# Order of the up and down products, preparation distance and number of tile places in a Fourier and mixture-of-experts kernel

## The chip, the core and the metric

The kernel runs on one core of one Trainium2 chip. The metric is the device time of one execution in microseconds. The core has five engines with a queue each: PE (matrix products; PEld are its weight loads), ACT and DVE (elementwise work and the emptying of the product banks), POOL (elementwise work, and the issue of the indirect gathers and scatters) and SP (which here only issues DMAs). Each engine takes its own instructions strictly in the order in which the program lists them, and engines wait for each other through semaphores.

## What is computed

```python
X = np.fft.rfft(x, axis=1)                      # x: 8 x 2496 x 256
Yr = Xr @ w_r - Xi @ w_i + b_r
Yi = Xr @ w_i + Xi @ w_r + b_i
Yr, Yi = soft_threshold(Yr, 0.01), soft_threshold(Yi, 0.01)
y = np.fft.irfft(Yr + 1j * Yi, n=2496, axis=1)  # 19968 tokens of 256
e_idx = np.argmax(y @ w_gate, axis=1)           # 8 experts
for e in range(8):
    mask = e_idx == e
    h = np.maximum(y[mask] @ w1[e], 0.0)        # 256 -> 1024
    out[mask] = gate_w[mask, None] * eom[mask, e, None] * (h @ w2[e])
```

## The kernel before

The Fourier part works through the eight sequences one after another: two stages of the forward transform, the mixing with the weights, two stages of the inverse, whose rows go to a DRAM buffer `yd`. Its last product stages are line 761 (first inverse stage, reads `zhl`) and line 827 (last inverse stage, reads `bdt`, the transposed `bt`; its results pass through `yt` and are stored by line 847).

The expert part works on tiles of 128 tokens that share an expert. There are 163: tiles 0 to 63 come from the first four sequences and are paired, 32 blocks of two tiles of one expert; tiles 64 to 162 are blocks of one tile. A tile goes through these steps, each with its line:

- `gathers`, line 1327: POOL issues an indirect gather of the tile's rows into a place `yg`.
- `tokens`, lines 1343 to 1353: DVE and ACT scale the rows and split them into two 16-bit parts in a place `yhl`.
- `tokens`, line 1366: SP issues a DMA transpose of `yhl` into a place `eT`. This ends what is called preparing a tile.
- `up`, line 1458: PE multiplies with the expert's first matrix, in pieces; ACT (1468) and DVE (1469) empty each piece into `hh`.
- `down`, line 1424: PE multiplies with the second matrix; ACT (1440) empties the product into `o`, and POOL scatters it (1443).

Expert weights lie in three buffers `wbuf`, which the blocks use in turn (the first four blocks use two). `fetch`, line 1313, has SP issue two DMAs of 1 MB for every block: the first part (for `up`) once the up product of the block three before is done, the second (for `down`) once the down product of that block is done. Both are conditional: a register that SP reads first (line 1310) says whether the buffer already holds this expert, and then the DMA moves nothing. So most tiles load nothing, and at a change of expert three blocks in a row load both parts.

The order on every engine is written by a planner (`Issue`): coroutines ask for an engine with a priority, which is the second item of what they yield, and of those that are ready in the plan the lowest goes first. `Slots` and `Places` are counted resources: a coroutine waits in the plan until one is free, and the real waits (semaphores) follow from the memory that the instructions touch. `AHEAD` holds a tile's preparation back in the plan until the up product of the tile so many before is planned. `down` for a single tile asks for PE with priority 4 after its tile's `up`, where the next tile's `up` stands at 5.6.

Of the kernel before, what the change touches and what calls it, by code (L numbers as in the profile page):

```python
# [13 lines left out]
F16 = mybir.dt.float16  # L14
F32 = mybir.dt.float32
# [9 lines left out]
B, S, D, E, DF = 8, 2496, 256, 8, 1024  # L25
N = B * S
N1, N2, K1 = 39, 64, 20
NQ = 22
P3 = 3 * N1
NCOL = B * NQ  # L30
ROW = 260
LAM = 0.01
XR = 6
# [3 lines left out]
T_A = -((-(NA * S - E * 255)) // 256) * 2  # L37
# [107 lines left out]
TAIL = 1.7  # L145
# [3 lines left out]
PLACES = dict(yg=6, yhl=5, eT=3, hh=2, o=5)  # L149
UP, DN = 2.8, 1.4  # L150
AHEAD = 6
KW = 4
YR, ZR, AN, WR, SR = 2, 3, 6, 3, 6
S1 = 6
# [15 lines left out]
OL = 2, 3  # L170
# [115 lines left out]
def tile_fft_moe(ctx, tc, x, w_r, w_i, b_r, b_i, w_gate, w_og, w1, w2, f1, f4, cmat, gmat, m16, out, dbg=None):  # L286
    nc = tc.nc
# [146 lines left out]

    bt = pf.tile([128, 4 * NQ, 128], F16, name="bt")
    G.memset(bt[:, :, 120:], 0.0)

    ste = pf.tile([128, 2, 2, 120], F32, name="ste")
    G.memset(ste, 0.0)
    bdt = py.tile([128, 4 * NQ, 128], F16, name="bdt")  # L440
    at = pm.tile([128, K1, 2, 2, 128], F16, name="at")
# [9 lines left out]
    io = Issue(list(range(8)))  # L451
    slots = {k: Slots(n) for k, n in dict(x=XR - 6, s1=S1, A=AN, xt=3, z=2, zhl=ZR, bt=1, bd=1, yt=YR, ol0=OL[0], wr=WR - 1, wsp=SR, ol1=OL[1], fac=12, dg=1, gL=1).items()}
    slots.update({k: Places(range(EARLY[k])) for k in EARLY})
# [3 lines left out]
    def move(r, nbytes, issue, fn):  # L457

        yield "S", r, max(issue, nbytes / RATE), fn
# [817 lines left out]
    def open_h():  # L1277
# [6 lines left out]
        for k, n in PLACES.items():  # L1284
            for i in range(EARLY[k], n):
                io.put(slots[k], i)

    def place(k, i, shape, dt):
        return pools["w" if i < EARLY[k] else "h"].tile(shape, dt, tag=f"{k}{i}", name=f"{k}{i}")

# [7 lines left out]
    def fetch(r):  # L1298

        yield "w open"  # L1300
        for k, (t, n) in enumerate(BLOCKS):
            yield "plan", 0 if t < T_A else 1
            if k == KW:
                yield "opened"
            for m in range(2):
                if before(k) is not None:
# [22 lines left out]

    facs = psm.tile([128, 18], F32, name="facs")  # L1330
    yms = psm.tile([128, 8], F32, name="yms")

    def tokens(t, iy, yg, r):

        il = yield slots["yhl"]
        yield slots["fac"]
        if t >= AHEAD:
            p = t - AHEAD
            yield "up", p - p % 2 if p < T_A else p
        m = yms[:, t % 8:t % 8 + 1]  # L1340
        fac = facs[:, t % 18:t % 18 + 1]
        yhl = place("yhl", il, [128, 2, 256], F16)
# [10 lines left out]
        yield "D", r - 10, 0.48, lambda: V.scalar_tensor_tensor(yhl[:, 1], yg[:, :256], s, yhl[:, 0], ALU.mult, ALU.subtract)  # L1353
        io.put(slots["yg"], iy)
        if t >= T_A:
# [9 lines left out]
        eT = st["eT", t][1][:, t % 2 if t < T_A else 0]  # L1365
        yield from move(r - 10, 1.4e5, 1.2, lambda: nc.sync.dma_start(eT.rearrange("p v c n -> p (v c) n"), yhl.rearrange("p v d -> p (v d)"), transpose=True))
        st["fac", t] = fac
        yield TAIL
        io.put(slots["yhl"], il)
        io.set("eT", t)  # L1370
# [9 lines left out]
    def back(k, t, i):  # L1380

        if t >= T_A:
            io.put(slots[k + "1"], i)
            return
        st["n" + k] = st.get("n" + k, 0) + 1
        if st["n" + k] <= T_A // 2 - PLACES[k]:
            io.put(slots[k], i)
        else:
            for h in range(2):
                io.put(slots[k + "1"], (i, h))  # L1390

    def block(k, r):
# [18 lines left out]
        for i in range(m):  # L1411
            io.go(down(t + i, m, i, w, hh, ih, r + (11.2 + 2 * UP * i + DN if m > 1 else 4)))

    def down(t, m, n, w, hh, ih, r):
# [28 lines left out]
        yield "G", r - DN, 1.0, lambda: G.indirect_dma_start(out=outs[t % 8], out_offset=bass.IndirectOffsetOnAxis(ap=sidx[:, t:t + 1], axis=0), in_=o, in_offset=None, bounds_check=N - 1, oob_is_err=False)  # L1443
        yield 3.6
        io.put(slots["o"], io_)
# [48 lines left out]
    io.go(open_w())  # L1494
    io.go(open_h())
    io.go(fetch(P * B + RT + WF))
    io.go(gathers(P * B + RT))
# [28 lines left out]
```

## Time and profile before

| | us |
|---|---|
| median of three timed runs | 1444.25 |
| the three runs | 1444.25, 1450.45, 1444.25 |
| profiled execution, own time | 1450.28 |
| span of the profiled execution | 1448.5 |
| PE busy in it | 1402.4 |
| DVE, ACT, POOL busy in it | 978.5, 737.0, 636.1 |
| first up product starts at | 552.01 |
| up products of single tiles from about | 907 |

The span is from the first to the last instruction of that execution; its own time is 1.78 us longer. Engine rows of a timeline give the start, the duration, the line, the operation, the tiles and a count; in square brackets the idle time ahead of the row and what ended it. A PE row's duration runs some 0.16 us into the row behind it, since products overlap; the time that a row occupies is the distance to the next row's start.

### The profile page before, as it was taken

To read this page: it belongs to the slowest core of one execution; us is meant where nothing else is said; L and a number is where in the kernel's file an instruction comes from. 1 tells how busy PE (TensorE), PEld (TensorE's weight loads), DVE (VectorE), ACT (ScalarE), POOL (GpSimd) and SP (SyncE) were. 2 spreads that over 40 slices of the span, in tenths; PEclk is the share of its full clock that TensorE was granted. 3 is DMA by queue.
4 is the path that set the end of the run, shared out by engine and by line. 5 is a ranking of instruction groups with operands and counts; after the bars stand their busy time and mean duration, and the time that the engine had idled before them with its cause. 6 is when DMAs were issued, how large, how long until landed. Compare 5 with 4: busy or idle time off the path is not lost.

```text
span 1448.5 us, 42626 instructions
## 1 busy us (share of the span) xinstructions
PE 1402.4 (97%) x16436; PEld 1273.4 (88%) x16436; DVE 978.5 (68%) x2796; ACT 737.0 (51%) x1413; POOL 636.1 (44%) x729
## 2 busy tenths in 40 slices
PE   4999999999999999999999999999999999999998
PEld 4998887888888888888888888999999999989998
DVE  4888767788998896788888855545545455445452
ACT  4777675778687764433333333333333333333342
POOL 2274565355577563345554333333343333333321
PEclk8999999999999999999999999999999999999999
DMA  7779899998988789977795789674838568386520
GB/s 197 174 174 217 205 224 211 220 223 216 218 211 202 177 238 197 285 193 199 232 231 145 215 207 264 168 218 111 245 94 227 160 167 242 81 244 194 126 58 24
DMA packets 294005, 276.47 MB, mean 191 GB/s; under 512 B 241847, under 2 KB 250169, under 8 KB 282026
## 3 DMA queue, kind: packets, MB, share of 16 engines
q1 hardware_dynamic: 277239, 229.68, 62.5%
q0 software_dynamic: 15872, 42.83, 12.3%
q8 instruction: 129, 2.11, 0.6%
q10 hardware_dynamic: 690, 1.24, 0.3%
q14 instruction: 75, 0.61, 0.1%
HBM read 337.44 MB, written 58.91 MB: 274 GB/s over the span
## 4 chain that ended last, share of the span: by engine, by line
PE 45%; issue 29%; POOL 14%; DVE 6%; DMA 2%; ACT 2%; SPq 1%; POOLq 0%; ACTq 0%; DVEq 0%
PE ps L731 11%; PE ps L1458 9%; PE ps L1424 8%; POOL out L1443 7%; POOL yg L1327 7%; PE ps L623 5%; PE ps L761 3%; PE ps L827 3%; PE ps L701 3%; DMA x<-in_x 1%; PE ps L872 1%; PE ps L666 1%; PE ps L725 1%; PE ps L1253 1%; DVE z L747 1%
## 5 line engine op out<-in xcount | busy, mean ns | idle before, releaser
L1458 PE MATMUL ps<-eT,wbuf 128*128 128x128 f16 (+1 forms) x6288 | 460.9, 233 | 8.4 <-DMA wbuf<-wd 5.6
L1424 PE MATMUL ps<-wbuf,hh 128*128 128x256 f16 x3912 | 453.8, 273 | 0.6 <-DMA wbuf<-wd 0.6
L1458 PEld LDWEIGHTS <-wbuf 128*128 128x128 f16 x6288 | 419.2, 98 | 30.0 <-DMA wbuf<-wd 7.2
L1424 PEld LDWEIGHTS <-hh 128*128 128x128 f16 x3912 | 378.9, 98 | 45.7 <-issue 1.3
L1469 DVE SCALAR_TENSOR_TENSOR hh<-ps,hh 128x512 f16<-128x512 f32 x326 | 224.9, 690 | 275.8 <-ACT hh L1468 275.6
L1468 ACT ACTIVATE hh<-ps 128x512 f16<-128x512 f32 x326 | 194.6, 597 | 294.3 <-PE ps L1458 287.9
L1443 POOL DMA_INDIRECT out<-o,sidx x163 | 163.4, 1003 | 283.4 <-ACT o L1440 259.7
L1327 POOL DMA_INDIRECT yg<-yd,gidx x163 | 161.5, 991 | 252.4 <-DVE yhl L1353 218.2
L731 PE MATMUL ps<-whl,xt 128*128 128x256 f16 x1920 | 223.1, 273 | 0.7 <-ACT xt L716 0.7
L731 PEld LDWEIGHTS <-xt 128*128 128x128 f16 x1920 | 187.6, 98 | 32.2 <-ACT xt L716 1.1
L1440 ACT ACTIVATE o<-ps,facs 128x256 f32<-128x256 f32 x163 | 77.2, 473 | 229.1 <-PE ps L1424 138.4
L1353 DVE SCALAR_TENSOR_TENSOR yhl<-yg,ys,yhl 128x256 f16<-128x256 f32 x163 | 81.8, 508 | 66.2 <-ACT yhl L1352 66.1
L623 PEld LDWEIGHTS ps<-f1t,x 117*128 117x128 f32 (+1 forms) x704 | 86.4, 199 | 18.2 <-issue 15.9
L623 PE MATMUL ps<-f1t,x 117*128 117x120 f32 (+1 forms) x704 | 89.9, 284 | 0.2 <-ACT ste L778 0.2
L1352 ACT ACTIVATE yhl<-yg,ys 128x256 f16<-128x256 f32 x163 | 81.7, 501 | 13.9 <-DVE ys L396 6.2
L751 POOL TENSOR_TENSOR zhl<-z,zhl 128x512 f16<-128x512 f32 x54 | 62.7, 1162 | 52.4 <-ACT zhl L749 50.0
L1028 POOL TENSOR_TENSOR wsp<-wr,wsp 128x512 f16<-128x512 f32 x62 | 74.3, 1198 | 5.2
L761 PE MATMUL ps<-gt,zhl 128*128 128x128 f16 x960 | 65.7, 220 | 7.9 <-DVE zhl L751 3.4
L761 PEld LDWEIGHTS <-zhl 128*128 128x128 f16 x960 | 58.6, 98 | 15.0 <-DVE zhl L751 4.2
L827 PE MATMUL ps<-bdt,f4t 120*117 120x512 f16 x264 | 70.6, 383 | 0.1
L632 ACT ACTIVATE at<-ps,sx 128x480 f16<-128x480 f32 (+1 forms) x88 | 55.7, 650 | 29.1 <-PE ps L623 25.9
L633 DVE SCALAR_TENSOR_TENSOR at<-ps,sx,at 128x480 f16<-128x480 f32 (+1 forms) x88 | 59.3, 696 | 12.5 <-ACT at L632 12.3
(195 smaller groups left out, 1647.8 us busy)
## 6 DMA issues: line engine op xcount, KB each, us to landing
wbuf<-wd SPq DMA_DIRECT2D x262, 1024.0 KB
yd<-yt SPq DMA_DIRECT2D x120, 158.4 KB
x<-in_x SPq DMA_DIRECT2D x114, 156.0 KB
wr<-in_moe_w SPq DMA_DIRECT2D x32, 512.0 KB
wd<-wsp SPq DMA_DIRECT2D x64, 256.0 KB
yg<-yd,gidx POOLq DMA_INDIRECT x163
eT<-yhl SPq DMA_TRANSPOSE x163
out<-o,sidx POOLq DMA_INDIRECT x163
```

The source lines that it names most:

```text
L623: T.matmul(pv[:, dh, :, m * j:m * j + m], xs[:k, j0 + j, 128 * dh:128 * dh + 128], fw, start=True, stop=True)
L731: T.matmul(yp[:, 256 * j:256 * j + 256], xt_[:, v, 2 * dh + j, 64 - 64 * u:192 - 64 * u], whl[:, dh, vw, 256 * u:256 * u + 256], start=Fal ...
L761: T.matmul(bv[:, j], zhl[:, vz, c:c + 128], gt[:, 2 * p + j, v], start=(n == 0), stop=(n == 2))
L827: T.matmul(pt[:P3], w, src[:, :, :, vb_], start=(n == 0), stop=(n == 2))
L1327: yield "G", r + 5.6 * t - 30, 1.0, lambda: G.indirect_dma_start(out=yg, out_offset=None, in_=src, in_offset=bass.IndirectOffsetOnAxis(ap= ...
L1352: yield "A", r - 10, 0.5, lambda: A.activation(yhl[:, 0], yg[:, :256], AF.Copy, scale=s)
L1353: yield "D", r - 10, 0.48, lambda: V.scalar_tensor_tensor(yhl[:, 1], yg[:, :256], s, yhl[:, 0], ALU.mult, ALU.subtract)
L1424: T.matmul(st["pt", t][1][:, :256], hh[:, v, fc, 128 * n:128 * n + 128], w[:, fc // 2, vw, fc % 2], start=(fc == k == 0), stop=(fc == 7 an ...
L1443: yield "G", r - DN, 1.0, lambda: G.indirect_dma_start(out=outs[t % 8], out_offset=bass.IndirectOffsetOnAxis(ap=sidx[:, t:t + 1], axis=0), ...
L1458: T.matmul(pt[:, 128 * m * j:128 * m * (j + 1)], w[:, dh, g // 4, vw, 128 * (g % 4):128 * (g % 4) + 128], eT[:, :m, v, dh], start=(n == 0) ...
L1468: yield "A", r, 0.6, lambda: A.activation(hv[:, 0], pt, AF.Relu)
L1469: yield "D", r, 0.69, lambda: V.scalar_tensor_tensor(hv[:, 1], pt, 0.0, hv[:, 0], ALU.max, ALU.subtract)
```

## The change

It does four things. A single tile's down product gets priority 8 in place of 4, behind the next tile's up product and ahead of that of the tile after it. The distance at which tiles are prepared, 6 before, becomes 8 for tiles 0 to 27, 14 for tiles 28 to 63 and 12 for the single tiles. The Fourier part's `bt` and `bdt` are reused, once the last inverse transform has been stored, as 13 more places for `yg`, 8 for `yhl`, 6 for `eT` and 8 for `o` (`open_late`). And a few rules of the plan change: the second block's weights are asked for only when the second tile is prepared, the transposes of the first four tiles get an early priority, and places are given back in the plan a little later.

```diff
-AHEAD = 6
+AHEAD = 8, 8, 14, 12
+LATE = dict(yg=13, yhl=8, eT=6, o=8)
+FAR = 28
...
+    def open_late():
+        yield "ys", B - 1, 5
+        yield "btr", B - 1
+        yield "lbm", B - 1
+        yield "opened"
+        room = []
+        for pool, tag in ((pf, "bt"), (py, "bdt")):
+            room.append((pool.tile([128, 4 * NQ * 128], F16, tag=tag, name="late" + tag), [0]))
+        for k, size in (("o", 512), ("yhl", 512), ("eT", 1024), ("yg", 2 * ROW)):
+            for i in range(PLACES[k], PLACES[k] + LATE[k]):
+                w, at_ = next(x for x in room if x[1][0] + size <= 4 * NQ * 128)
+                late[k, i] = w[:, at_[0]:at_[0] + size]
+                at_[0] += size
+                io.put(slots[k], i)
...
             if k == KW:
                 yield "opened"
+            if k == 1:
+                yield "eT", 1
...
-        if t >= AHEAD:
-            p = t - AHEAD
+        p = t - AHEAD[2 * (t >= FAR) + (t >= T_A)]
+        if p >= 0:
             yield "up", p - p % 2 if p < T_A else p
...
-        io.put(slots["yg"], iy)
+        io.at(io.now + (4 if t > 11 else 0), io.put, slots["yg"], iy)
...
-        yield from move(r - 10, 1.4e5, 1.2, lambda: nc.sync.dma_start(eT..., yhl..., transpose=True))
+        yield from move(r - (10 if t > 3 else 70), 1.4e5, 1.2, lambda: nc.sync.dma_start(eT..., yhl..., transpose=True))
...
-            io.go(down(t + i, m, i, w, hh, ih, r + (11.2 + 2 * UP * i + DN if m > 1 else 4)))
+            io.go(down(t + i, m, i, w, hh, ih, r + (11.2 + 2 * UP * i + DN if m > 1 else 8)))
...
-        yield 3.6
+        yield 8.0
         io.put(slots["o"], io_)
```

What this does to the order shows at three places. First ACT among the single tiles. Its rows stand for PE's products: two rows of line 1468 (1495 in the changed kernel) empty one tile's up product, one row of 1440 (1467) a down product; 1352 (1379) prepares a tile. Before:

```order
L1468 ACTIVATE hh0_9904<-ps1_16894 128x512
L1468 ACTIVATE hh0_9904<-ps4_16921 128x512
L1352 ACTIVATE yhl1_16946<-yg4_16236,ys4_16972 128x256
L1468 ACTIVATE hh0_9904<-ps6_16977 128x512
L1440 ACTIVATE o0_17073<-ps0_17006,facs_146 128x256
L1352 ACTIVATE yhl2_17031<-yg5_16349,ys5_17043 128x256
L1440 ACTIVATE o1_17128<-ps7_17048,facs_146 128x256
```

And in the changed kernel, in the same part of the program:

```order
L1495 ACTIVATE hh1_9953<-ps6_16454 128x512
L1495 ACTIVATE hh1_9953<-ps7_16486 128x512
L1379 ACTIVATE latebt_11351<-yg4_15365,ys7_16563 128x256
L1467 ACTIVATE o4_16598<-ps4_16532,facs_146 128x256
L1495 ACTIVATE hh1_9953<-ps1_16573 128x512
L1495 ACTIVATE hh1_9953<-ps3_16605 128x512
L1379 ACTIVATE latebt_11351<-yg5_15412,ys0_16682 128x256
L1467 ACTIVATE latebt_11351<-ps2_16651,facs_146 128x256
```

Up products came two in a row and then two down products; now one up product, one down product, and the down product is that of the tile before.

Second SP among the single tiles: `DMA wbuf` are a block's two weight DMAs, first part and second part, `TENSOR_LOAD` the reading of the condition ahead of a first part, `DMA_TRANSPOSE` a tile's transpose; the brackets hold what an instruction waits for. Before, from the second part of one tile on (the transposes' tiles are some three ahead of the weights'):

```order
L1313 DMA wbuf2_9430<-wd_79 128x4096 [waits DMAHW6_49,PE_49]
L1310 TENSOR_LOAD ebi_5952
L1310 ISA x2
L1310 TENSOR_LOAD flg_5951
L1310 ISA x2
L1313 ISA
L1313 DMA wbuf0_9304<-wd_79 128x4096 [waits DMAHW7_49]
L1366 DMA_TRANSPOSE eT0_9665<-yhl4_17271 128x4x128 [waits DMAHW0_49,DVE_49]
L1313 ISA
L1313 DMA wbuf0_9304<-wd_79 128x4096 [waits DMAHW1_49,PE_49]
```

And in the changed kernel:

```order
L1340 DMA wbuf1_9305<-wd_79 128x4096 [waits DMAHW7_49,PE_49]
L1393 DMA_TRANSPOSE latebdt_11352<-latebt_11351 128x4x128 [waits DMAHW0_49,DVE_49]
L1337 TENSOR_LOAD ebi_5952
L1337 ISA x2
L1337 TENSOR_LOAD flg_5951
L1337 ISA x2
L1340 ISA
L1340 DMA wbuf2_9430<-wd_79 128x4096 [waits DMAHW1_49]
L1340 ISA
L1340 DMA wbuf2_9430<-wd_79 128x4096 [waits DMAHW3_49,DMAHW2_49,PE_49]
```

Before, every first part stood directly behind the second part of the block before it, with the transpose behind both. Now the tile's transpose stands between the second part of a block and the first part of the next, and a block's two parts stand together, the first with no wait for PE of its own.

Third SP at the start of the expert part: the stores of the seventh sequence (`yd`), the first transposes and the weights of the second block (`wbuf1`). Before:

```order
L1313 DMA wbuf1_9305<-wd_79 128x4096 [waits DMAHW0_49]
L1366 DMA_TRANSPOSE eT0_9665<-yhl0_9552 128x4x128 [waits DMAHW1_49,DVE_49]
L1313 ISA
L1313 DMA wbuf1_9305<-wd_79 128x4096 [waits DMAHW2_49]
L847 DMA yd_78<-yt0_133 39x1040 [waits DMAHW3_49,Activation_49,Pool_49]
L847 DMA yd_78<-yt0_133 39x1040 [waits DMAHW4_49]
L847 DMA yd_78<-yt0_133 39x1040 [waits DMAHW5_49]
L847 DMA yd_78<-yt1_134 39x1040 [waits DMAHW6_49,Activation_49,Pool_49]
L847 DMA yd_78<-yt1_134 39x1040 [waits DMAHW7_49]
L847 DMA yd_78<-yt1_134 39x1040 [waits DMAHW0_49]
L1366 DMA_TRANSPOSE eT0_9665<-yhl1_9559 128x4x128 [waits DMAHW1_49,DVE_49]
```

And in the changed kernel:

```order
L1393 DMA_TRANSPOSE eT0_9646<-yhl0_9552 128x4x128 [waits DMAHW0_49,DVE_49]
L849 DMA yd_78<-yt0_133 39x1040 [waits DMAHW1_49,Activation_49,Pool_49]
L849 DMA yd_78<-yt0_133 39x1040 [waits DMAHW2_49]
L849 DMA yd_78<-yt0_133 39x1040 [waits DMAHW3_49]
L1393 DMA_TRANSPOSE eT0_9646<-yhl1_9559 128x4x128 [waits DMAHW4_49,DVE_49]
L849 DMA yd_78<-yt1_134 39x1040 [waits DMAHW5_49,Activation_49,Pool_49]
L849 DMA yd_78<-yt1_134 39x1040 [waits DMAHW6_49]
L849 DMA yd_78<-yt1_134 39x1040 [waits DMAHW7_49]
L1393 DMA_TRANSPOSE eT1_9750<-yhl2_9581 128x4x128 [waits DMAHW0_49,DVE_49]
L1393 DMA_TRANSPOSE eT1_9750<-yhl3_9622 128x4x128 [waits DMAHW1_49,DVE_49]
```

The second tile's transpose passes three stores and the second block's weights, which now follow the fourth transpose. On PE the first three pieces of `up` move ahead of the last product of line 761, with two products of line 827 between them.

More of the change, by code (lines that the diff above doesn't have):

```diff
@@ L433, in tile_fft_moe @@
     junk = px.tile([128, 1024], mybir.dt.bfloat16, name="junk")
-    bt = pf.tile([128, 4 * NQ, 128], F16, name="bt")
+    bt = pf.tile([128, 4 * NQ, 128], F16, tag="bt", name="bt")
     G.memset(bt[:, :, 120:], 0.0)
@@ L439, in tile_fft_moe @@
     G.memset(ste, 0.0)
-    bdt = py.tile([128, 4 * NQ, 128], F16, name="bdt")
+    bdt = py.tile([128, 4 * NQ, 128], F16, tag="bdt", name="bdt")
     at = pm.tile([128, K1, 2, 2, 128], F16, name="at")
@@ L451, in tile_fft_moe @@
     io = Issue(list(range(8)))
-    slots = {k: Slots(n) for k, n in dict(x=XR - 6, s1=S1, A=AN, xt=3, z=2, zhl=ZR, bt=1, bd=1, yt=YR, ol0=OL[0], wr=WR - 1, wsp=SR, ol1=OL[1], fac=12, dg=1, gL=1).items()}
+    slots = {k: Slots(n) for k, n in dict(x=XR - 6, s1=S1, A=AN, xt=3, z=2, zhl=ZR, bt=1, bd=1, yt=YR, ol0=OL[0], wr=WR - 1, wsp=SR, ol1=OL[1], fac=20, dg=1, gL=1).items()}
     slots.update({k: Places(range(EARLY[k])) for k in EARLY})
@@ L1286, in open_h @@
                 io.put(slots[k], i)
-    def place(k, i, shape, dt):
+    late = {}
+    def open_late():
[12 more added lines that the diff above has]
+                io.put(slots[k], i)
+    def place(k, i, shape, dt):
+        if i >= PLACES[k]:
+            w = late[k, i] if dt == F16 else late[k, i].bitcast(dt)
+            if len(shape) == 2:
+                return w
+            names = "abcd"[:len(shape) - 1]
+            return w.rearrange(f"p ({' '.join(names)}) -> p {' '.join(names)}", **dict(zip(names, shape[1:])))
         return pools["w" if i < EARLY[k] else "h"].tile(shape, dt, tag=f"{k}{i}", name=f"{k}{i}")
@@ L1328, in gathers @@
             io.go(tokens(t, i, yg, r + 5.6 * t), io.now + 2.6)
-    facs = psm.tile([128, 18], F32, name="facs")
+    facs = psm.tile([128, 28], F32, name="facs")
     yms = psm.tile([128, 8], F32, name="yms")
@@ L1336, in tokens @@
         yield slots["fac"]
-        if t >= AHEAD:
-            p = t - AHEAD
+        p = t - AHEAD[2 * (t >= FAR) + (t >= T_A)]
+        if p >= 0:
             yield "up", p - p % 2 if p < T_A else p
         m = yms[:, t % 8:t % 8 + 1]
-        fac = facs[:, t % 18:t % 18 + 1]
+        fac = facs[:, t % 28:t % 28 + 1]
         yhl = place("yhl", il, [128, 2, 256], F16)
@@ L1365, in tokens @@
         eT = st["eT", t][1][:, t % 2 if t < T_A else 0]
-        yield from move(r - 10, 1.4e5, 1.2, lambda: nc.sync.dma_start(eT.rearrange("p v c n -> p (v c) n"), yhl.rearrange("p v d -> p (v d)"), transpose=True))
+        yield from move(r - (10 if t > 3 else 70), 1.4e5, 1.2, lambda: nc.sync.dma_start(eT.rearrange("p v c n -> p (v c) n"), yhl.rearrange("p v d -> p (v d)"), transpose=True))
         st["fac", t] = fac
+        io.at(io.now + (6 if t > 11 else TAIL), io.put, slots["yhl"], il)
         yield TAIL
-        io.put(slots["yhl"], il)
         io.set("eT", t)
@@ L1385, in back @@
         st["n" + k] = st.get("n" + k, 0) + 1
-        if st["n" + k] <= T_A // 2 - PLACES[k]:
+        if st["n" + k] <= T_A // 2 - PLACES[k] - LATE.get(k, 0):
             io.put(slots[k], i)
@@ L1495, in tile_fft_moe @@
     io.go(open_h())
+    io.go(open_late())
     io.go(fetch(P * B + RT + WF))
```

## The prediction

> **What bounds the kernel now.** I read the busy shares first.
>
> ```profile
> span 1448.5 us, 42626 instructions
> PE 1402.4 (97%) x16436; PEld 1273.4 (88%) x16436; DVE 978.5 (68%) x2796; ACT 737.0 (51%) x1413; POOL 636.1 (44%) x729
> ```
>
> PE is busy 1402.4 of 1448.5 us. The change adds and removes no product, so it can win only what PE lacks, 46 us over the whole span, and can lose without limit. Next I read what ended PE's waits from 541 us on, where the order first differs (columns: total us, count, longest).
>
> ```profile
> PE ps L1458 <- DMA wbuf<-wd: 5.6, 5, 2.2
> PE ps L761 <- ACT zhl L749: 3.0, 1, 3.0
> ...
> PE ps L1458 <- DMA eT<-yhl: 2.7, 1, 2.7
> ...
> PE ps L1424 <- DMA wbuf<-wd: 0.6, 1, 0.6
> ```
>
> Five waits of an up product for weights, one of a down product, one for a transposed tile, and a wait at the entrance. Then I read how PE spends a tile in an undisturbed stretch of the single tiles.
>
> ```profile
> 1009.15 5.52 PE L1458 MATMUL ps<-eT,wbuf 128*128 128x128 f16 x96
> 1014.51 5.40 PE L1424 MATMUL ps<-wbuf,hh 128*128 128x256 f16 x48
> 1019.75 5.52 PE L1458 MATMUL ps<-eT,wbuf 128*128 128x128 f16 x96
> ```
>
> Two up products occupy 1014.51 - 1009.15 = 5.36 us, two down products 1019.75 - 1014.51 = 5.24. That is 2.68 and 2.62 each, 5.30 a tile, with no gap and no operand late. **Taking turns saves nothing where nothing waits.** The change can act in four places: the entrance, the wait for a transposed tile, the region of tile 64, and the changes of expert among the single tiles.
>
> **The entrance.** PE's rows from 541 on, and SP's and DVE's beside them:
>
> ```profile
> 541.33 0.79 PE L761 MATMUL ps<-gt,zhl 128*128 128x128 f16 x11 [0.35 <-POOL zhl L751]
> 545.13 0.29 PE L761 MATMUL ps<-gt,zhl 128*128 128x128 f16 x1 [3.01 <-ACT zhl L749]
> 546.22 1.35 PE L761 MATMUL ps<-gt,zhl 128*128 128x128 f16 x11 [0.80 <-DVE zhl L751]
> ...
> 552.01 6.72 PE L1458 MATMUL ps<-eT,wbuf 128*128 128x256 f16 x60
> ```
>
> ```profile
> 540.00 4.73 SPq L847 DMA_DIRECT2D yd<-yt  x6
> 544.83 5.95 SPq L1366 DMA_TRANSPOSE eT<-yhl  x4
> ...
> 539.78 0.47 DVE L1353 SCALAR_TENSOR_TENSOR yhl<-yg,ys,yhl 128x256 f16<-128x256 f32 x1
> ...
> 540.76:552.01 11.25, 7.03 (x99) 5.01 (x98) 9.07 (x30) 6.66 (x16) 5.86 (x9) 0.70 1.08 270
> ```
>
> The first up product starts at 552.01, behind all of line 761. In these 11.25 us PE was busy 7.03 at a granted clock of 0.70, and it waited 0.35 + 3.01 + 0.80 = 4.16. At full clock those 7.03 would be between 0.70 x 7.03 = 4.9 and 7.03; I take 5.5 (the low clock lay mostly behind the long wait), so at most 11.25 - 5.5 = 5.7 can be won. In the new order three up pieces stand ahead of the last of line 761. They need the second tile's transpose. Its `yhl` is ready at 539.78 + 0.47 = 540.25, but SP issued it behind six stores, after 544.83. Now three stores (half of 4.73 us) stand ahead of it: issue near 542.5, two us sooner. The up pieces can then fill part of the 3.01 wait and all of the 0.80, and they keep the clock up. I take **-3.7**, between 0 (the transpose is late there as well) and -5.7.
>
> **The wait for a transposed tile.**
>
> ```profile
> 853.34 4.16 PE L1458 MATMUL ps<-eT,wbuf 128*128 128x256 f16 x24 [2.72 <-DMA eT<-yhl]
> 857.30 1.80 PE L1424 MATMUL ps<-wbuf,hh 128*128 128x256 f16 x12
> 858.94 1.47 PE L1458 MATMUL ps<-eT,wbuf 128*128 128x256 f16 x12
> ```
>
> PE waited 2.72 us, and then its clock was low: 24 products took 857.30 - 853.34 = 3.96 us where the 48 down products above (of the same 256 columns) took 2.62, so 24 should take the 2 x 1.31 = 2.62 that two groups of 12 take; and the next 12 took 1.64 in place of 1.31. That is 1.34 + 0.33 = 1.67 more, 4.4 in all. Tiles 28 to 63 are now prepared 14 ahead and not 6, eight tiles of some 5.3 us, so a transpose that was 2.72 late is not late any more. I take **-4.4**, with 0 if the places do not let the preparation run ahead.
>
> The preparation that catches up is paid on DVE:
>
> ```profile
> 600.00:700.00 100.00, 99.14 (x927) 87.48 (x925) 81.93 (x243) 39.36 (x76) 47.00 (x53) 1.00 0.79 219
> ```
>
> DVE, third of the engines in this row, is busy 81.9 of 100 us here. While the distance grows by eight tiles its pieces can come ahead of the emptying of `up`'s banks. I take **+1**, from 0 to +5, the upper end being a tile's time.
>
> **The region of tile 64.**
>
> ```profile
> 925.48 2.85 PE L1458 MATMUL ps<-eT,wbuf 128*128 128x128 f16 x48 [0.70 <-DMA wbuf<-wd]
> 928.92 5.40 PE L1424 MATMUL ps<-wbuf,hh 128*128 128x256 f16 x48 [0.59 <-DMA wbuf<-wd]
> ```
>
> Two waits, 0.70 + 0.59 = 1.3. The last down piece of the paired blocks moves ahead of tile 66's up product, so that SP, which waits for that piece, issues the next weights a product sooner. I take **-1.3**, with 0 as the other end.
>
> **The changes of expert: the large term.** Among the single tiles the expert changes seven times (tiles 74, 86, 98, 110, 121, 133, 142). At each, three tiles load both parts, and the fifth load, the first part of the third tile, is what ends last. The first change in SP's rows, and PE's row at the fifth load of it and of three others:
>
> ```profile
> 952.93 2.26 SPq L1313 DMA_DIRECT2D wbuf<-wd  x2
> 955.30 1.23 SPq L1366 DMA_TRANSPOSE eT<-yhl  x1
> 956.89 2.25 SPq L1313 DMA_DIRECT2D wbuf<-wd  x2
> ...
> 977.34 5.53 PE L1458 MATMUL ps<-eT,wbuf 128*128 128x128 f16 x96 [0.53 <-DMA wbuf<-wd]
> ...
> 1201.36 2.37 SPq L1313 DMA_DIRECT2D wbuf<-wd  x2
> 1226.10 2.85 PE L1458 MATMUL ps<-eT,wbuf 128*128 128x128 f16 x48 [1.56 <-DMA wbuf<-wd]
> ...
> 1266.76 2.31 SPq L1313 DMA_DIRECT2D wbuf<-wd  x2
> 1292.08 2.85 PE L1458 MATMUL ps<-eT,wbuf 128*128 128x128 f16 x48 [2.21 <-DMA wbuf<-wd]
> ...
> 1318.78 1.91 SPq L1313 DMA_DIRECT2D wbuf<-wd  x2
> 1343.32 5.53 PE L1458 MATMUL ps<-eT,wbuf 128*128 128x128 f16 x96 [0.56 <-DMA wbuf<-wd]
> ```
>
> Each SP row is the last empty second part and the first real first part. From its end to the product that the fifth load releases: 977.34 - 955.19 = 22.15 us at tile 74; 22.37 at 121; 23.01 at 133; 22.63 at 142. The up products that waited are all five of the view above (the fifth is tile 64's); their waits at changes are 0.53 + 1.56 + 2.21 + 0.56 = 4.9, with the smaller ones some 5.2. The changes at 86, 98 and 110 have no such row: their five loads just came in time.
>
> Why five loads take so long shows in two stretches of the trace, the first a burst and the second quiet:
>
> ```profile
> 955.85:976.76 20.91, 20.91 (x283) 19.52 (x280) 11.05 (x36) 8.01 (x16) 7.55 (x9) 1.00 1.08 310
> ...
> 930.00:950.00 20.00, 20.00 (x278) 19.02 (x277) 9.13 (x31) 7.73 (x15) 6.93 (x7) 1.00 0.34 74
> ```
>
> In a burst the DMA engines are full (1.08) at 310 GB/s: five loads of 1.05 MB and the tiles' own traffic. The time is set by transfer, about 20.9 / 5 = 4.2 us a load, not by when each was issued.
>
> Now the new order. Call Y the end of the down product of the tile four before the change. SP's second part of the tile ahead waits for it, moves nothing, and then come the transpose (1.23) and the first real part, whose issue ends at about Y + 2.3 + 1.2 + 0.2 = Y + 3.7. The fifth load is needed by the up product of the tile two behind the change. Between Y and it PE has four up and four down products: 4 x 5.30 = 21.2 us. So the window is 21.2 - 3.7 = **17.5 us**. Before, it was 22.15 - 0.53 = 21.6 at tile 74: pairs put two down products together, and the first part was asked for behind the up product of the pair before.
>
> A burst that does not change is then late by 22.15 - 17.5 = 4.65 at tile 74 and 5.1 at 142. At 121 and 133 the DMA engines stood idle a us or two between the first two loads, which the new order fills: 3 to 5. At 86, 98 and 110, which were in time, it is at most 21.7 - 17.5 = 4.2 and I put the least at 2. Mean 3.6, times seven 25.2, less the 5.2 of before: **+20**. The bounds: with bursts of 19 us it is 7 x 1.5 - 5.2 = +5; with 22.5, 7 x 5 - 5.2 = +30.
>
> **The clock behind these waits.** A wait of 2.72 us was followed by a half clock and 1.67 us more (853.34 above); one of 2.21, at 1292.08, was not, as its 48 products end in the 2.85 us of every such row. New waits of 2 to 4.6 us lie on both sides. I count three of seven, 3 x 1.67 = **+5**, from 0 to 11.7. The Trainium skill, page "TensorE: Matmul & The Clock Gate", section "Part 1: The HAM clock gate", has the clock fall only after a whole idle window of some 3.4 us; the trace disagrees at 853.34, where 2.72 sufficed. By that page most of these waits would cost no clock.
>
> **The sum,** against the profiled execution's own 1450.28: -3.7 - 4.4 - 1.3 + 20 + 5 + 1 = +16.6, so 1466.9. That execution is 6.0 over the median of the runs shown (1444.25, in two of three; the third, 1450.45, is like it). Nothing in its rows says what the 6.0 is; I take off two thirds, as two of three runs were without it: 1466.9 - 4 = **1463**.
>
> **Rivals.**
> - *The burst is only partly late.* For it: loads now start evenly and never all at once. Bursts of 19 us give 1450.28 - 9.4 + 1 + 5 = 1447, less 4 at most: 1443 to 1447, no change. Chance 0.16.
> - *Faster: the loads get the DMA engines to themselves.* Twelve tiles ahead, gathers and transposes may give way in a burst. Five loads alone, 5.24 MB at 310 GB/s, are 16.9 us, under the window of 17.5. Then the waits of before go, too: 1450.28 - 9.4 - 5.2 = 1435.7, with 1 or 2 lost elsewhere 1437, less the shift 1433. Against it: a tile needs one transpose and one gather each 5.30 us however far ahead, and the quiet stretch shows that these take a share of 0.34, so 0.34 x 17.5 = 6 us of the window. It decides where the fifth load lands within 17.5 us of the first one's issue. Chance 0.11. The Trainium skill, page "DMA: Bandwidth & Descriptors", section "Where 436 GB/s comes from", names about 358 GB/s as the limit from HBM for a core; by it five loads alone would take 14.6 us, and this rival would have more room.
> - *No half clock behind the waits.* 1463 - 5 = 1458; slower all the same. Chance 0.10.
> - *A half clock behind all seven.* 1463 - 5 + 11.7 = 1470. Chance 0.05.
> - *The places come too late or wait for each other,* so that preparation is no farther ahead and the wait at 853 stays, with the DMA reading reused memory late: 1463 + 4.4 + 4 = 1471. For it: the late memory opens only once the last inverse transform is stored. Chance 0.05.
>
> **How the numbers follow.** The forecast has 0.53. A measurement of this kernel can tell about 0.5% from no change, that is outside 1437.0 to 1451.5. The faster rival gives 0.11, the partly late burst 0.16 within, and the rest, 0.73, slower. The range reaches from 1440, leaving out the faster rival, to 1480: the sum with the upper burst (+10) and all seven half clocks (+7) is 1463 + 17.
>
> **What would show it.** Right: seven waits of up products for `wbuf` of 2 to 5 us each in the trace of the changed kernel, about 25 in all; no wait for `eT` near 853; first up product near 544, then line 761's end without 3 us of idle time; waits at tile 64 gone; granted clock below 1 behind the longest waits. Wrong: the fifth load landing in less than 17.5 us from the first's issue, or SP's first part issued well before Y + 3.7, or DVE or ACT in PE's list of releasers with several us, from DVE's crowding.

## The result and the profile after

| | us | ratio to the kernel before | 95% interval |
|---|---|---|---|
| kernel before, 4 runs | 1446.8 | | |
| changed kernel, 4 runs | 1484.62 (1484.06 to 1487.97) | 1.0264 | 1.0232 to 1.0297 |
| forecast | 1463 (1440 to 1480) | | |

The change made the kernel slower, as forecast, but by 38 us and not by 16 to 19; the time lies above the range. The profiled execution of the changed kernel took 1484.06 us of its own, 33.8 more than that of the kernel before (1450.28).

The page of the changed kernel, its span and busy shares, and then what ended PE's waits from 541 us on (total us, count, longest):

```profile
span 1482.3 us, 42491 instructions
...
PE 1417.7 (96%) x16436; PEld 1287.3 (87%) x16436; DVE 970.5 (65%) x2793; ACT 745.1 (50%) x1413; POOL 638.6 (43%) x732
```

```profile
PE ps L1485 <- DMA wbuf<-wd: 23.1, 10, 4.1
PE ps L1485 <- DMA eT<-yhl: 7.9, 3, 3.3
PE ps L1255 <- POOL ob L1247: 5.4, 8, 1.7
PE ps L1485 <- ACT yt L833: 1.7, 1, 1.7
```

Up products (1485, 1458 before) now wait 23.1 us for weights where they waited 5.6. PE does the same 16436 products and is busy 15.3 us longer: that is a lower clock, 0.983 of full speed over the whole span where it was 0.993, some 25 us lost to it in place of 10. The waits for transposed tiles have grown from 2.7 to 7.9 us, those for `ob` (operands of the second routing's products, 1255) from 0.7 to 5.4, and the wait for `yt` is new.

Where the 33.8 us arise shows when both kernels are at the same product of PE (start in us of the n-th product in the two traces; the order is the same up to about 541 us in the kernel before, and almost the same work lies ahead of each later number):

```
product   before    after     after - before   added since the row above
 5600     512.67    507.97     -4.7             -4.7
 8000     766.26    775.76     +9.5            +14.2
 9200     899.55    903.92     +4.4             -5.1
 9600     934.38    935.86     +1.5             -2.9
16435    1443.98   1477.76    +33.8            +32.3
```

The -4.7 is a difference of two executions, since up to there the order is the same. The single tiles lose most. Their ideal is 5.30 us a tile; what each change of expert adds to it, measured as the time from the down product three tiles before it to that five tiles behind it, less 8 x 5.30:

```
                               74     86     98    110    121    133    142    sum
before                        0.8    0.0    0.1    0.4    1.7    2.4    0.9    6.4
changed                       6.0    5.0    5.8    4.9    6.9    4.1    4.7   37.5
```

There is no loss anywhere else among the single tiles: from tile 66 to tile 160 it is 37.46 in all. Of these the profile gives 23.1 as waits; some 12.3 are products that took longer in stretches of half clock, and the rest, some 2 us, is the overlap of products that each wait takes away (ten times 0.16) and gaps too short for the view. The first change in PE's and SP's rows of the changed kernel:

```profile
952.87 2.78 PE L1451 MATMUL ps<-wbuf,hh 128*128 128x256 f16 x24
955.49 2.84 PE L1485 MATMUL ps<-eT,wbuf 128*128 128x128 f16 x48
...
968.77 2.78 PE L1451 MATMUL ps<-wbuf,hh 128*128 128x256 f16 x24
974.65 5.30 PE L1485 MATMUL ps<-latebt,wbuf 128*128 128x128 f16 x48 [3.10 <-DMA wbuf<-wd]
979.75 3.13 PE L1451 MATMUL ps<-wbuf,hh 128*128 128x256 f16 x24
982.72 2.84 PE L1485 MATMUL ps<-latebt,wbuf 128*128 128x128 f16 x48
```

```profile
954.01 1.75 SPq L1340 DMA_DIRECT2D wbuf<-wd  x2
955.86 1.29 SPq L1393 DMA_TRANSPOSE latebt<-yhl  x1
958.99 2.35 SPq L1340 DMA_DIRECT2D wbuf<-wd  x2
961.43 1.25 SPq L1393 DMA_TRANSPOSE latebdt<-yhl  x1
964.23 2.39 SPq L1340 DMA_DIRECT2D wbuf<-wd  x2
```

The first real load stands in the row at 958.99, 3.5 us after the down product that the empty second part ahead of it waits for had ended (Y, at 955.49, where the next product starts). The product at 974.65 is the up product of tile 75: it waits for the **third** load, not the fifth. It then runs at half clock (48 products in 5.1 us), and tile 76's follows at 982.72 with no wait of its own.

### The profile page after: what moved, and what is told of

Its sections match the earlier page's. It is cut to its first block, busy times and chain, and to the rows that moved or that the text cites. A ratio compares the mean times of both kernels' runs of the same rounds, so it can differ in the third digit from the quotient of the medians.

```text
span 1482.3 us, 42491 instructions
## 1 busy us (share of the span) xinstructions
PE 1417.7 (96%) x16436; PEld 1287.3 (87%) x16436; DVE 970.5 (65%) x2793; ACT 745.1 (50%) x1413; POOL 638.6 (43%) x732
## 4 chain that ended last, share of the span: by engine, by line
PE 25%; issue 22%; POOL 7%; DMA 2%; DVE 1%; SPq 0%; POOLq 0%; ACT 0%; ACTq 0%
PE ps L1485 13%; PE ps L1451 12%; POOL out L1470 3%; POOL latebdt L1354 2%; DMA wbuf<-wd 1%; POOL yg L1354 1%; PE ps L1255 1%; POOL ob L1247 0%; DVE hh L1496 0%; DMA yd<-yt 0%; ACT hh L1495 0%; SPq L1393 0%; POOLq L1470 0%; DVE latebt L1380 0%; SPq L1337 0%
## 5 line engine op out<-in xcount | busy, mean ns | idle before, releaser
L1485 PEld LDWEIGHTS <-wbuf 128*128 128x128 f16 x6288 | 434.0, 100 | 58.8 <-DMA wbuf<-wd 29.4
L1470 POOL DMA_INDIRECT out<-latebt,sidx x93 | 92.5, 995 | 305.5 <-ACT latebt L1467 294.2
L1485 PE MATMUL ps<-eT,wbuf 128*128 128x128 f16 (+1 forms) x2448 | 199.3, 241 | 20.5 <-DMA wbuf<-wd 10.9
L1470 POOL DMA_INDIRECT out<-o,sidx x70 | 70.5, 1007 | 201.2 <-ACT o L1467 185.2
L1485 PE MATMUL ps<-latebt,wbuf 128*128 128x128 f16 (+1 forms) x1920 | 141.1, 234 | 6.0 <-DMA wbuf<-wd 6.0
L1485 PE MATMUL ps<-latebdt,wbuf 128*128 128x128 f16 (+1 forms) x1920 | 140.1, 233 | 6.2 <-DMA wbuf<-wd 6.2
L1354 POOL DMA_INDIRECT latebdt<-yd,gidx x95 | 93.6, 985 | 27.8 <-issue 23.9
L1467 ACT ACTIVATE latebt<-ps,facs 128x256 f32<-128x256 f32 x93 | 44.0, 473 | 101.1 <-PE ps L1451 100.0
L1354 POOL DMA_INDIRECT yg<-yd,gidx x68 | 67.3, 989 | 33.9 <-issue 13.9
L634 ACT ACTIVATE at<-ps,sx 128x480 f16<-128x480 f32 (+1 forms) x88 | 55.7, 649 | 28.7 <-PE ps L625 26.1
L1467 ACT ACTIVATE o<-ps,facs 128x256 f32<-128x256 f32 x70 | 33.1, 473 | 70.5 <-PE ps L1451 70.5
```

The source lines that it names most:

```text
L1354: yield "G", r + 5.6 * t - 30, 1.0, lambda: G.indirect_dma_start(out=yg, out_offset=None, in_=src, in_offset=bass.IndirectOffsetOnAxis(ap= ...
L1467: yield "A", r - DN, 0.47, lambda: A.activation(o, pt[:, :256], AF.Copy, scale=fac)
L1485: T.matmul(pt[:, 128 * m * j:128 * m * (j + 1)], w[:, dh, g // 4, vw, 128 * (g % 4):128 * (g % 4) + 128], eT[:, :m, v, dh], start=(n == 0) ...
```

## The experiments

Times are compared with the kernel before on the same chip.

**1. Turns undone in the changed kernel.**

```diff
-            io.go(down(... (11.2 + 2 * UP * i + DN if m > 1 else 8)))
+            io.go(down(... (11.2 + 2 * UP * i + DN if m > 1 else 4)))
```

> The changed kernel with the single tiles' down product back at priority 4, so that two up products and then two down products follow each other; farther preparation, the late places and the entrance stay. Theory A (turns leave 17.5 us for five loads that take some 21, and a half clock follows each long wait): the seven changes of expert wait some 6 us in all again, with no half clock behind them, so 1484.6 - 31 = 1453 (1450 to 1457). Rival B (gathers and transposes that run 12 tiles ahead take the DMA engines from the loads, whatever the order of products): the seven waits stay at 2 to 4 us, 1475 or more.

1458.35, ratio 1.0079 (1.0056 to 1.0103). The seven changes lose 10.2 us, not 37.5. Theory A, with a time a little above the expected 1450 to 1457: the changes at 121 and 133 still lose 3.3 and 6.5.

**2. Turns alone**, the same number from 4 to 8 in the kernel before.

> The kernel before with the single tiles' down product at priority 8 and nothing else. Theory A: seven waits of 2 to 4 us at the changes of expert and a half clock behind most of them, 19 + 12 us on 1446.8, so 1478 (1472 to 1481). Rival B: the waits stay at some 6 us in all, 1445 to 1450.

1477.71, ratio 1.0212 (1.0172 to 1.0251). The seven changes lose 37.3 us, with a half clock at each. Both sides of theory A hold: the turns alone make the loss, whatever the preparation.

**3. Preparation 6 ahead.**

```diff
-AHEAD = 8, 8, 14, 12
+AHEAD = 6, 6, 6, 6
```

> The changed kernel with every tile prepared 6 ahead as before; turns, late places and the entrance stay. Theory C (the 13 late places for gathered rows open at once, POOL issues gathers one behind the other from 636 to 680 us, and PE waits for the products `ob` of the second routing that stand behind them on POOL): the places still let gathers run ahead, since the distance holds back only what follows a gather, so these waits (some 7 us) stay, and the wait for a transposed tile near 850 comes back with its half clock, 4.4: 1489 (1486 to 1492). Rival (the distance makes them): the 7 us go, the 4.4 come back, 1482 (1479 to 1485). Either way the seven waits at the changes stay at 20 us or more under theory A; under rival B they fall to 8 or less, 1470.

1484.62, ratio 1.0243 (1.0209 to 1.0277). The time lies in the rival's range and not in theory C's. The changes lose 36.9. PE's waits for `ob` are 3.5 us in place of 5.4 from 541 us on, so the distance takes part in them; what is left of them, with the distance undone, is not shown to come of the places alone. The wait for a transposed tile near 850 does **not** come back: what stands there is 1.33 us at 859.45, which the profile puts down to weights. The distance alone moves the time by nothing that can be measured.

**4. The two entrance rules undone.**

```diff
-            if k == 1:
-                yield "eT", 1
...
-        yield from move(r - (10 if t > 3 else 70), ...
+        yield from move(r - 10, ...
```

> The changed kernel without its two rules for the entrance (the second block's weights wait for the second tile, and the early priority of the first four transposes). Theory D (these rules are what makes up products wait 1.9 and 2.6 us for transposed tiles near 589 and 604, with a half clock behind the second): those 6 us go and the 3 us wait of line 761 comes back in place of the 3.3 us wait at 538, so 1478 (1475 to 1480). Rival (the longer distance brings those waits, as its transposes crowd SP's queue and the DMA engines): no difference, 1483 to 1487.

1473.4, ratio 1.0171 (1.0133 to 1.0208): 11 us less than the changed kernel had, more than expected. PE no longer waits for a transposed tile, and the wait of 3.0 us of the first inverse stage is back. Between products 5600 and 8000 it loses 2.4 us to the kernel before, not 14.2, and between 8000 and 9600 it gains 8.0. SP's last transposes of the eighth sequence (`bdt`) in the kernel before, in the changed kernel and in this one:

```profile
576.93 3.53 SPq L801 DMA_TRANSPOSE bdt<-bt  x2
```

```profile
597.45 1.22 SPq L1393 DMA_TRANSPOSE eT<-yhl  x1
...
599.58 7.07 SPq L803 DMA_TRANSPOSE bdt<-bt  x1
```

```profile
571.37 6.05 SPq L803 DMA_TRANSPOSE bdt<-bt  x3
```

They end at 580.5, 606.7 and 577.4 us. In the changed kernel they stand between the tiles' transposes. That this makes those late, and the last inverse transform, its stores and the second routing behind them, is theory G, taken up in runs 14 and 15.

**5. The first part ahead of the second part of the block before**, in the changed kernel, among the single tiles.

```diff
-        for k, (t, n) in enumerate(BLOCKS):
...
-            for m in range(2):
...
+        steps = [(k, m) for k in range(len(BLOCKS)) for m in range(2)]
+        for k in range(T_A // 2 + 1, len(BLOCKS) - 1):
+            a = steps.index((k, 1))
+            steps[a], steps[a + 1] = steps[a + 1], steps[a]
+        for k, m in steps:
```

> The changed kernel with SP's order of the single tiles' weights altered: each block's first part is issued ahead of the second part of the block before it, so it waits for an up product one place earlier on PE and passes one transpose. In the changed kernel the first wait at six of the seven changes is that of the second new tile (its first part is the third load), not of the third new tile. Theory E (the third load is issued too late and shares the DMA engines with the fourth; the place in the queue decides): the waits at the changes fall from 25 us to 5 or less with no half clock behind them, 1484.6 - 31 = 1454 (1450 to 1462). Rival (five loads take 21 us of transfer in any order): the wait moves to a later load and stays at 2 us or more at each change, 1470 or more.

1469.15, where the kernel before took 1462.66 on this chip: ratio 1.005 (1.0028 to 1.0072), 2.1% below the changed kernel's. The seven changes lose 1.0 us and no half clock is left. Theory E.

**6. Products that fill the waits**, in the changed kernel.

```diff
             pt = bank(i)
+            if half == 0 and t in (75, 87, 99, 111, 122, 123, 134, 144):
+                for _ in range(32):
+                    T.matmul(pt[:, :128], eT[:, 0, 0, 0], eT[:, 0, 0, 0], start=True, stop=True)
```

> The changed kernel with 32 products of 128x128 (32 x 0.056 = 1.8 us), on data that is long there and into the bank that the up product overwrites, ahead of the up products that wait at the changes (tiles 75, 87, 99, 111, 122, 123, 134, 144 of these inputs). They lie inside waits of 2.2 to 4.2 us, so no wait ends later. Theory F (the clock is halved where PE was idle for over 2.1 us of one of the fixed stretches of 3.41 us that the clock's changes lie on): idle falls to 0.4 to 2.4 us, at most one of seven half clocks is left, 12 to 14 us less: 1471 (1469 to 1476). Rival (the half clock comes of something else that the waits have, such as full DMA engines, or the products are not hidden): no gain, 1483 to 1499.

1515.08, ratio 1.0352 (1.0313 to 1.0391): no gain, as the rival has it. It ran on the chip of run 5, beside products that waited for what the profile calls `issue`, so it was repeated as run 12.

**7. The new order of the weights in the kernel before.**

> The kernel before with that order of the single tiles' weights and nothing else. Theory E: its waits at changes (6 us, at tiles 76, 123, 135, 144) fall below 1 us, 1446.2 - 5 = 1441 (1438 to 1444). Rival: they stay or move to a down product, 1445 or more.

1464.52, ratio 1.0018 (1.0002 to 1.0034). No gain: the waits moved to down products (tiles 75, 99, 111, 123, 143: 1.3 to 2.8 us), and the seven changes lose 22.0 us, waits for `issue` (below) among them. The order suits turns and not products two and two, which use both second parts of a pair ahead of the next first part.

**8. Farther preparation, two and two, the new order**, no entrance rules.

> The changed kernel without its entrance rules and with the single tiles' products two and two again (priority 4), but with farther preparation and the late places, and with the new order of the weights. Farther preparation gave 5.7 us net up to the single tiles in the run without the entrance rules (the waits near 850 and tile 64 gone, some 2.4 us of waits for `ob` paid), and the order of the weights gives the 5 of the run beside this: 1446.2 - 10.7 = 1435.5 (1432 to 1441). Rival (farther preparation costs at the single tiles what it gave before them, as two long waits at 123 and 135 in the run with the turns undone suggest): 1442 or more.

1529.65, ratio 1.0458 (1.0425 to 1.0491): far from the forecast, and in the rival's open range for another reason than the rival's. One row of PE's waits in it from 535 us on:

```profile
PE ps L1489 <- issue: 45.8, 92, 1.2
```

In this row PE waited 45.8 us with nothing late that the profile knows (`issue`). Run again on another chip (13 below) these waits were gone. This first run says nothing of the kernel.

**9. The changed kernel with the new order and without the entrance rules.**

> The changed kernel with the new order of the weights and without its entrance rules; turns, farther preparation and late places stay. With the new order the waits at the changes were 1 us in all in the run that kept the entrance rules, and leaving these out saved 11 us. Theory E and D together: 5.7 us net won up to the single tiles and 5 at the changes, so 10 below the kernel before on the same chip, a ratio of 0.993 (0.989 to 0.997). Rival (the last run's 20 us over this sum, small waits inside products that the profile puts down to `issue`, belong to the kernel and not to that chip): 1.00 or more.

1439.6, ratio 0.9938 (0.9919 to 0.9958): faster than the kernel before. The seven changes lose 0.0 us. The first change in SP's and PE's rows:

```profile
945.14 2.03 SPq L1344 DMA_DIRECT2D wbuf<-wd  x2
...
950.42 2.32 SPq L1344 DMA_DIRECT2D wbuf<-wd  x2
```

```profile
946.90 2.84 PE L1489 MATMUL ps<-latebt,wbuf 128*128 128x128 f16 x48
...
962.80 2.84 PE L1489 MATMUL ps<-latebt,wbuf 128*128 128x128 f16 x48
965.48 2.78 PE L1455 MATMUL ps<-wbuf,hh 128*128 128x256 f16 x24
968.10 2.84 PE L1489 MATMUL ps<-latebt,wbuf 128*128 128x128 f16 x48
970.78 2.78 PE L1455 MATMUL ps<-wbuf,hh 128*128 128x256 f16 x24
```

The down product Y ends at 946.90, and the row with the first real load starts 1.8 us ahead of that, where in the changed kernel it started 3.5 behind. The up products of tiles 75 and 76 (962.80, 968.10) wait for nothing. The fifth load is now a second part, wanted at 970.78, so five loads have 25.6 us. The edit does two things at once: the first load is asked for some 5.3 us earlier, and the parts are asked for in the order of their use. No run takes the two apart; run 7 shows only that the new order gains nothing under products two and two.

**10. Turns and the new order in the kernel before**, nothing else.

> The kernel before with turns (priority 8) and the new order of the weights, nothing else. In this order the parts are loaded in the order in which turns use them: no wait at a change over 1 us, 5 us below the kernel before, a ratio of 0.9965 (0.994 to 0.999). Rival (turns cost something of their own at every tile): 1.002 or more, in 5.30 us a tile that has grown.

1439.19, ratio 0.9935 (0.9909 to 0.9961). The changes lose 0.7 us. Turns cost nothing of their own, and beside run 9 the farther preparation, the 35 places and the other rules are in sum worth nothing that can be measured (in the traces run 9 loses 4.3 us between products 5600 and 8000 and gains 5.1 from 8000 to 9200, run 10 does neither).

**11. The changed kernel again**, beside runs 9, 10 and 12.

> The changed kernel itself, as the measure for the runs beside it: a ratio of 1.0264 as before if chips agree, and waits that the profile puts down to `issue` only if they come of the chip.

1478.25, ratio 1.0217 (1.0178 to 1.0257). The changes lose 31.6 us here, with a half clock behind four of their five waits of over 2 us: the loss differs by some 6 us between these two executions, which were on different chips.

**12. The filled waits again.**

> The kernel with 32 added products ahead of the waiting up products, now beside the changed kernel on one chip. In its first run the part from tile 70 on grew by 21 us over the kernel before where the changed kernel's grew by 32, but the parts ahead of it were slower, with `issue` waits that no other chip had shown. Theory F: 8 to 13 us below the changed kernel run beside it, with two to three half clocks left at the changes. Rival: not below it.

1492.53, ratio 1.0324 (1.0277 to 1.0372): 14 us **above** run 11, as the rival has it. Tiles 75 and 76 in run 11 and in this one:

```profile
972.83 4.48 PE L1485 MATMUL ps<-latebt,wbuf 128*128 128x128 f16 x48 [3.07 <-DMA wbuf<-wd]
977.15 2.78 PE L1451 MATMUL ps<-wbuf,hh 128*128 128x256 f16 x24
980.04 2.85 PE L1485 MATMUL ps<-latebt,wbuf 128*128 128x128 f16 x48
```

```profile
971.86 1.95 PE L1482 MATMUL ps<-latebt 128*128 128x128 f16 x32
975.47 2.85 PE L1488 MATMUL ps<-latebt,wbuf 128*128 128x128 f16 x48 [1.66 <-DMA wbuf<-wd]
978.16 2.78 PE L1451 MATMUL ps<-wbuf,hh 128*128 128x256 f16 x24
983.71 2.85 PE L1488 MATMUL ps<-latebt,wbuf 128*128 128x128 f16 x48 [2.76 <-DMA wbuf<-wd]
```

Here the filling did what it was for: it lies inside the wait, and tile 75's products run at full clock (2.85 us, not 4.48). But tile 76 then waits 2.76 us for the fifth load. The half clock had lain in that wait's time: what the clock's return gives, the next load takes. In all, though, four half clocks are left at the changes (at tiles 88, 99, 111 and 135), as many as in run 11, so no run shows loads that come late without any half clock. Why the loads land even later with the filling (tile 100's up product 29.4 us after Y, 27.1 in run 11) is open.

A half clock behind the **last** wait of a change shares its time with nothing. The changed kernel at tiles 122 and 123:

```profile
1245.25 2.85 PE L1485 MATMUL ps<-eT,wbuf 128*128 128x128 f16 x48 [2.84 <-DMA wbuf<-wd]
1252.80 4.48 PE L1485 MATMUL ps<-eT,wbuf 128*128 128x128 f16 x48 [2.08 <-DMA wbuf<-wd]
1257.12 2.78 PE L1451 MATMUL ps<-wbuf,hh 128*128 128x256 f16 x24
1259.74 2.84 PE L1485 MATMUL ps<-eT,wbuf 128*128 128x128 f16 x48
```

Tile 124's up product follows 6.94 us behind tile 123's and not 5.30, with no wait between: 1.64 us that are the clock's alone. Tile 144 is the same.

**13. Run 8 again.**

> The kernel with farther preparation, products two and two, no entrance rules and the new order of the weights, once more. If the waits put down to `issue` belong to the chip of its first run, they are gone and it takes 1.000 to 1.012 of the kernel before (its waits at changes 5 to 20 us, since two and two do not use the parts in the order in which they are loaded). If they belong to the kernel, it takes 1.03 or more again with some 90 such waits.

1454.95, ratio 1.004 (1.0025 to 1.0056), with no wait for `issue`; the changes lose 11.0 us, and PE waits for second parts:

```profile
PE ps L1455 <- DMA wbuf<-wd: 11.7, 5, 3.2
```

**14. The rule on the second block's weights undone**, and **15. the early priority of four transposes undone**: each one half of run 4's edit.

> The changed kernel without the rule that the second block's weights wait for the second tile; the early priority of the first four transposes stays. On SP eight and more of the tiles' transposes still stand ahead of the eighth sequence's last six, as in the changed kernel. Theory G (that place of the eighth sequence's transposes makes the waits near 589 and 604): no gain, 1.021 to 1.027 of the kernel before. Rival (the late weights of the second block make them): 8 us or more less, 1.017 or below.

> The changed kernel without the early priority of the first four transposes; the rule on the second block's weights stays. On SP the eighth sequence's transposes stand behind 8 to 12 of the tiles', one later than in the changed kernel and before the run with both rules undone. Theory G: some of the waits stay, 1.018 to 1.026 of the kernel before. Rival (the early priority alone makes them, by way of the up products that it puts ahead of line 763): 11 us less, 1.015 to 1.018.

1484.61, ratio 1.0244 (1.0225 to 1.0263), and 1483.22, ratio 1.0237 (1.0199 to 1.0276): no gain from either alone. The eighth sequence's last transposes of runs 14 and 15:

```profile
584.25 5.93 SPq L803 DMA_TRANSPOSE bdt<-bt  x1
```

```profile
587.68 11.33 SPq L803 DMA_TRANSPOSE bdt<-bt  x1
```

They end at 590.2 and 599.0, and both runs lose 13.4 us between products 5600 and 8000, the changed kernel 14.2; the runs whose last such transpose ends at 577 and 580 us (4 and 9) lose 2.4 and 4.3. The changed kernel's second execution (run 11) loses 11.4. Theory G fits these runs as two groups: with that transpose at 590 us or later 11 to 14 us are lost, with it at 581 or earlier 1 to 4, leaving out the chip of runs 5 to 8; within a group a later end does not cost more. That these transposes are the cause was not tried by moving them alone.

## Why the prediction was wrong, step by step

| term | forecast | measured in the two profiles |
|---|---|---|
| entrance, and DVE's crowding | -3.7 + 1 | +14.2 (products 5600 to 8000) |
| wait for a transposed tile | -4.4 | -5.1 (8000 to 9200) |
| region of tile 64 | -1.3 | some -1.7 (what is left of the sum) |
| changes of expert, and the clock there | +20 + 5 | +31.1 (6.4 to 37.5) |
| offset of the profiled execution | -4 | -4.7 |

**Right: the main mechanism.** Turns shorten the time that five loads have, the loads take as long as before, and PE waits at all seven changes. Runs 1, 2, 9 and 10 show it from four sides. The waits at the changes rose from 4.9 to 23.1 us, by 18.2, where 20 was forecast. The waits at tile 64 went as forecast too (runs 4 and 9).

**Right in size, wrong in its cause: the late transposed tile.** -4.4 was put on the preparation 14 tiles ahead, and -5.1 came. But run 3, 6 ahead and with the late places, has no such wait either and keeps 3.6 of the 5.1, while the four kernels without the late places (the kernel before, runs 2, 7 and 10) all have one near 852, of 1.2 to 2.9 us. It goes with the late places, or with the rules that came with them, and not with the distance; that the number fitted was luck.

**Wrong: "the fifth load ... is what ends last".** At all seven changes the first wait is that of the third load. PE waits 0.8 to 4.1 us for it, and three times it waits again at the next tile, for the fifth (0.86, 2.08 and 1.99 us at tiles 112, 123 and 144). The sum came out near all the same: the up product that uses the fifth load stands on average 26.1 us behind Y in the changed kernel (24.3 to 27.2), that is 22.4 behind the issue's end at Y + 3.7, inside the 22.15 to 23.01 of the kernel before. At the four other changes this product has no wait of its own; that the fifth load would have held it up there too is argued from run 12, where it waits 2.35 to 2.76 us at each of the four, but where the loads also land later. Forecast was 24.8, because at tiles 86, 98 and 110 the least was put at 2 us; these three lose 4.9 to 5.8, as much as the others.

**Wrong: "I count three of seven" half clocks.** It was seven of seven, with products some 12.3 us longer (four, and some 6.5 us, in run 11). But the rival "a half clock behind all seven" would have been wrong in its price as well: it adds the clock to the waits, and run 12 shows at tile 76 that the two can share one time. The step that failed is to price waits and clock apart. Counted by place the changes come out so: the up product of the fifth load starts 26.1 us behind Y where 21.2 would do, so 4.9 late on average and 34.2 over the seven, and the half clocks behind the last wait at tiles 123 and 144 add 3.3: together the 37.5. The forecast had 25.2 (seven times 3.6) and 5, so the lateness was the term sized too small.

**Wrong, and the largest: the entrance, "I take -3.7, between 0 ... and -5.7".** The rules brought +14.2 with what follows, and run 4 has it back to 2.4. Two things went wrong. The up pieces now waited themselves:

```profile
541.40 2.72 PE L1485 MATMUL ps<-eT,wbuf 128*128 128x256 f16 x12 [3.33 <-DMA eT<-yhl]
...
589.34 2.78 PE L1485 MATMUL ps<-eT,wbuf 128*128 128x256 f16 x24 [1.94 <-DMA eT<-yhl]
...
603.86 1.68 PE L1485 MATMUL ps<-eT,wbuf 128*128 128x256 f16 x12 [2.58 <-DMA eT<-yhl]
...
623.09 1.47 PE L1485 MATMUL ps<-eT,wbuf 128*128 128x256 f16 x12 [1.70 <-ACT yt L833]
```

The wait of 3.01 us of line 761 was not filled but replaced, by 3.33 for the second tile's transpose, and the half clock came with it as before. And the prediction read the order of SP for some ten rows at the entrance and not for those behind it, in which the eighth sequence's transposes end 26 us later. The later waits at 589, 604 and 623 are gone in run 4, and those for `ob` fall from 5.4 to 3.8; so these rules make them, and runs 14 and 15 show that either alone costs as much. By which of the moved transfers they do it is argued (theory G) and stays open.

**Wrong in kind: "+1" for DVE.** The crowding is on POOL. The stretch of 636 to 680 us before and after (PE, PEld, DVE, ACT, POOL busy, clock, DMA share, GB/s):

```profile
636.00:680.00 44.00, 43.19 (x419) 38.60 (x417) 36.88 (x99) 16.44 (x32) 23.22 (x25) 1.00 0.78 211
```

```profile
636.00:680.00 44.00, 38.60 (x364) 33.66 (x362) 39.06 (x116) 16.60 (x33) 36.15 (x38) 1.00 1.03 266
```

DVE goes from 36.9 to 39.1, POOL from 23.2 to 36.2: from 636.9 us on it issues gathers into the late places one behind the other, and the products of the second routing wait for POOL's `ob`. PE does 4.6 us less in these 44.

## What to carry to other kernels

An order in which every operand is on time gains nothing from being made more even; what counts is the least time between the request for a large transfer and its use, over all places where transfers come in a burst, and which of them is used first. The loads' order has to be changed with the products' order: turns alone lost 31 us, turns with the parts requested in the order of their use won 0.6%. And when a planner's rule moves one early instruction, the whole queue behind it is to be compared, to its end.

## What the runs showed of the hardware

The clock's changes lie on a fixed grid of 3.41 us, and what halves it is not the length of a wait but how much of it falls into one stretch of the grid. The idle time is counted here by the starts of the products, with their usual spacing taken as busy. In all 17 traces, from 100 us on, 106 stretches at full clock were followed by a half clock, and in each PE had stood idle for 2.04 us or more; 205 with idle time of 0.8 us or more were not, and in those it was 2.10 at most. So the wait of 2.84 us at tile 122, split by the grid, left the clock whole, and the one of 2.08 behind it did not. The four stretches of the changed kernel at tiles 122 and 123 (first PE's busy time, then the clock):

```profile
1243.27:1246.69 3.42, 1.44 (x26) 1.45 (x27) 0.00 (x0) 0.00 (x0) 1.90 (x2) 1.00 1.60 365
1246.69:1250.10 3.41, 3.41 (x46) 3.20 (x44) 2.48 (x9) 1.70 (x3) 0.00 (x0) 1.00 0.70 260
1250.10:1253.51 3.41, 1.33 (x19) 1.01 (x18) 0.28 (x1) 0.47 (x1) 1.70 (x2) 1.00 0.99 402
1253.51:1256.93 3.42, 3.42 (x36) 3.42 (x34) 1.21 (x4) 0.60 (x1) 0.27 (x1) 0.50 0.98 162
```

With 1.44 us busy the clock stays at 1.00, with 1.33 it is 0.50 in the next stretch. This also settles what the prediction weighed: the trace showed 2.72 us with and 2.21 without a half clock, and both follow from the grid: 2.2 us of the first wait lie in the stretch that ends at 854.55, and the second is cut at 1291.46 into 1.6 and 0.6. The Trainium skill, page "TensorE: Matmul & The Clock Gate", section "Part 1: The HAM clock gate", has free-running windows of that length, and the runs agree (3.41 us); it has the clock fall after an idle window, and here 2.04 to 2.10 of the 3.41 us idle are enough.

On one chip PE stood still again and again with nothing late that the profile knows (`issue`), for at most 0.4 us at a time in run 7 and up to 1.6 in run 5, and for some 57 us in all in run 8; the kernel before took 1462.66 there and 1446 to 1450 on the others. What makes it is open.
